# Compressive-memory attention on one core: the memory matrix in 32x32 blocks of two heads, q and k rows head by head

## The chip, the core and the metric

The kernel runs on one core of a Trainium2 chip. The metric is the device time of one execution in microseconds (us); lower is better. The core has a matrix engine (PE; PEld is its weight load), a vector engine (DVE), an activation engine (ACT), a general engine (POOL) and a sequencer that issues nearly all transfers (SP). The transfers run on 16 DMA engines.

## The reference, cut to what matters

One transformer block: adaptive layer norm, attention with a compressive memory, adaptive layer norm, a feed-forward network with GELU. 2048 rows, width 512, 32 heads of 16, four segments of 512 rows. The change touches only the attention.

```python
for s in range(4):                       # segments of 512 rows
    qs, ks, vs = q[:, :, s], k[:, :, s], v[:, :, s]
    a_dot = softmax(qs @ ks.T * scale + mask) @ vs       # within the segment
    pq = phi(qs)                                         # phi(t) = t + 1 if t > 0 else exp(t)
    num = einsum("bhld,bhde->bhle", pq, M)               # memory read-out, M is 16x16 a head
    den = einsum("bhld,bhd->bhl", pq, z)[..., None] + 1e-6
    o = g * num / den + (1 - g) * a_dot
    pk = phi(ks)
    M = M + einsum("bhld,bhle->bhde", pk, vs)            # memory update
    z = z + sum over l of pk
```

## The kernel before, in words

The program runs in three phases. Phase one, which the change touches, goes through the four segments: layer norm, projections to q, k and v, memory read-out and memory update. Phase two computes the dot-product attention of all heads and the output projection. Phase three is the feed-forward network.

**Order.** The order is written out by hand. For phase one it is the token lists `PRM['A']` (line 62), one for each segment, which the loop at line 531 turns into calls: `Q0` to `Q3` and `K0` to `K3` are projections of four groups of eight heads (128 rows: eight heads of 16) by 512 columns (the segment's rows); `R` is the read-out, `Rs`, `Rb`, `Rn`, `Ro` are the store of its reciprocal, the broadcast load of it, the multiplication and the store of the result; `Tk`, `Tc` and `U` transpose phi(k), copy it and update the memory. Segment 0 has no read-out. Each engine takes its instructions in the order in which the tokens emit them, and so does SP with its transfers. A transfer goes out on one of eight semaphore lanes in turn, so transfer n waits until transfer n-8 has landed.

**Projection** (`proj`, line 504). Twelve products on PE fill one PSUM bank of 128x512. ACT copies it, rounded, to a tile "hi" (line 516), DVE subtracts (line 517) and gives "lo"; each of the two has three buffers, so the copy of projection n waits until the stores of projection n-3 have landed. `store` (line 498) writes both to DRAM: hi goes to two planes of `QD` or `KD`, lo to the third. For the memory, ACT also makes exp (line 515), POOL or DVE clips it (line 520), and DVE joins the two halves of phi (line 526). The eight PSUM banks of the pool `psA` are used in turn by all tokens.

**Layout.** The columns of wq and wk are permuted on the host so that a group's row is `dim * 8 + head`. A plane of `QD[s][g]` in DRAM is `[dim 16][head 8][512]`, so hi and lo lie there exactly in the order of their 128 rows.

**Loads of phase two.** `load_stacks` (line 186) reads, for a "quad" Q of four heads, 48 rows of 4 KB for two of its heads at a time: two loads of k and two of q. A DRAM row of 4 KB is two neighbouring heads of one dim. The loads of quads 0 and 1 are emitted in segment 3 (token `B`), those of quad 2 right after the last store of phase one.

**Memory read-out** (`mem_read`, line 446). Four products give the denominators, four column blocks of 32 beside each other in one bank (`dn`, line 449). Then a product of 128 rows and 128 columns for each group g, with a 128x128 matrix M that is zero outside the blocks of its eight heads, gives the numerators in four banks (`nu`, line 457); ACT copies each to a tile `am`. DVE makes the reciprocals. `mem_store` writes them to DRAM (`rdd`), `mem_load` reads them back broadcast over 16 dims (`rb`, line 471), POOL multiplies (line 476), and `mem_out` stores the results to `AMD[s][g]` (line 480), from where phase two takes them.

**Memory update** (`mem_update`, line 426). For each group and each of four blocks of 128 rows a product of transposed phi(k) (128 columns) with 128 columns of V adds up in a bank `mp` (line 434); DVE multiplies with a mask of the heads (line 440) and adds the old M (line 443).

All of these memory products are in full fp32. The trace shows two weight loads and two products for each, so 16 products of `mp` are 32 rows in a segment.

Of the kernel before, what the change touches and what calls it, by code (L numbers as in the profile page):

```python
# [8 lines left out]
F32 = mybir.dt.float32  # L9
# [3 lines left out]
ALU = mybir.AluOpType  # L13
# [4 lines left out]
S, D, H, DH, NSEG, L, F = 2048, 512, 32, 16, 4, 512, 1792  # L18
# [4 lines left out]
VW = 17  # L23
# [81 lines left out]
def block_kernel(ctx: ExitStack, tc: tile.TileContext, x, wq, wk, wv, wo, betaq, betam,  # L105
                 w1, b1c, w2, b2, ccol, wmod, maskbd, mask8, out):
    nc = tc.nc
    v, act, pool, pe, sp = nc.vector, nc.scalar, nc.gpsimd, nc.tensor, nc.sync
# [3 lines left out]
    dram = ctx.enter_context(tc.tile_pool(name="dram", bufs=1, space=DRAM))  # L112
# [49 lines left out]

    QD = [[dram.tile([3, 16, 8, 512], F32, name=f"QD{s}_{g}") for g in range(4)] for s in range(NSEG)]
    KD = [[dram.tile([3, 16, 8, 512], F32, name=f"KD{s}_{g}") for g in range(4)] for s in range(NSEG)]
    TERMS = {"q": (slice(0, 3, 2), slice(1, 2)), "k": (slice(0, 2), slice(2, 3))}
    def home(Q):
        return Q % 5 if Q < 10 else (Q - 10) % 6

# [26 lines left out]
                    for p in range(2):  # L195
                        sp.dma_start(st[p][64 * h:64 * h + 48], rows[:, o + p, :])

    AMD = [[dram.tile([128, 512], F32, name=f"AMD{s}_{g}") for g in range(4)] for s in range(NSEG)]
    X2D = [dram.tile([128, 4, D], F32, name=f"X2D{s}") for s in range(NSEG)]
    GD = [[dram.tile([128, 512], F32, name=f"GD{s}_{f}") for f in range(FB)] for s in range(NSEG)]  # L200
    modD = dram.tile([6, D], F32, name="modD")
# [12 lines left out]
    V = [vp.tile([128, VROW], F32, tag="V", bufs=NB, name=f"V{b}") for b in range(NB)]  # L214
# [8 lines left out]
    with ExitStack() as pa:  # L223
        sa = pa.enter_context(tc.tile_pool(name="sa", bufs=2))
        wp = pa.enter_context(tc.tile_pool(name="wp", bufs=1))
        pp = pa.enter_context(tc.tile_pool(name="psA", bufs=8, space=PSUM))

        def pst(name):
            return pp.tile([128, 512], F32, tag="ps", name=name)

        def sat(tag, name, dt=F32):
            return sa.tile([128, 512], dt, tag=tag, bufs=PRM["bufs"][tag], name=name)
# [3 lines left out]
        def load_x(s):  # L236
            xs[s] = wp.tile([128, 4, D], F32, tag="xs", bufs=2, name=f"xs{s}")
            if s > 0:
                sp.dma_start(xs[s], xrows(s))
            else:  # L240
                for b in range(4):
                    (sp if b < 2 else act).dma_start(xs[0][:, b], xrows(0)[:, b])
# [32 lines left out]
        wvs = load_w(wvp, wv, "wv", "pkt")  # L275
        (wqh, wql), (wkh, wkl), (wvh, wvl) = wqs[:2], wks[:2], wvs[:2]
        load_x(1)
        mbd = wp.tile([128, 128], F32, name="mbd")
        m8 = wp.tile([128, 32], F32, name="m8")
        sp.dma_start(mbd, maskbd)  # L280
        sp.dma_start(m8, mask8)
# [55 lines left out]
        ps = pst("mpsa")  # L337
        for k in range(KB):
            for c in range(2):
                pe.matmul(ps[32 * c:32 * c + 32, :], sc[:, k:k + 1].to_broadcast([128, 32]), wms[c, k],  # L340
                          start=(k == 0), stop=(k == KB - 1))
        row = sat("pkt", "mrowa")
# [65 lines left out]

        mem = {"M": None, "z": None}
        phq, phk, zss, pks, mrd = {}, {}, {}, {}, {}  # L410
# [15 lines left out]
        def mem_update(s):  # L426
            z = zss[s]
            if mem["z"] is not None:
                v.tensor_tensor(out=z, in0=mem["z"], in1=z, op=ALU.add)
            mp = pst(f"mp{s}")  # L430
            for g in range(4):
                for b in range(4):
                    rhs = V[4 * s + b][:, VW * 8 * g:VW * 8 * g + VW * 8].rearrange("p (h c) -> p h c", c=VW)[:, :, :16]
                    pe.matmul(mp[:, 128 * g:128 * g + 128], pks[s][b][:, 128 * g:128 * g + 128], rhs,
                              start=(b == 0), stop=(b == 3))
            zm = sa.tile([128, 4, 32], F32, tag="zm", name=f"zm{s}")
            for g in range(4):
                v.tensor_scalar(zm[:, g, :], m8, z[:, g:g + 1], None, op0=ALU.mult)
            M = sa.tile([128, 4, 128], F32, tag="M", name=f"M{s}")
            v.tensor_tensor(out=M, in0=mp.rearrange("p (g n) -> p g n", g=4),  # L440
                            in1=mbd[:, :].unsqueeze(1).to_broadcast([128, 4, 128]), op=ALU.mult)
            if mem["M"] is not None:
                v.tensor_tensor(out=M, in0=M, in1=mem["M"], op=ALU.add)
            mem["M"], mem["z"], mem["zm"] = M, z, zm

        def mem_read(s):
            dn = pst(f"dn{s}")
            for g in range(4):
                pe.matmul(dn[32 * g:32 * g + 32, :], mem["zm"][:, g, :], phq[s, g], start=True, stop=True)
            rd = sa.tile([128, 512], F32, tag="rd", bufs=1, name=f"rd{s}")  # L450
            v.tensor_scalar(rd, dn, 1e-6, None, op0=ALU.add)
            v.reciprocal(out=rd, in_=rd)
            v.tensor_scalar(rd, rd, gm[:, 0:1], None, op0=ALU.mult)
            ams = []
            for g in range(4):
                ps = pst(f"nu{s}_{g}")
                pe.matmul(ps, mem["M"][:, g, :], phq[s, g], start=True, stop=True)
                am = sat("am" if s < 3 else "phk", f"am{s}_{g}")
                act.activation(am, ps, AF.Copy)
                ams.append(am)  # L460
            mrd[s] = [rd, ams, []]

        def mem_store(s):
            rdd = dram.tile([128, 512], F32, name=f"rdd{s}")
            sp.dma_start(rdd, mrd[s][0])
            mrd[s][0] = mem["r"] = rdd

        def mem_load(s):
            for g in range(4):
                rb = sat("pkt", f"rb{s}_{g}")  # L470
                sp.dma_start(rb, mrd[s][0][32 * g:32 * g + 8, :].unsqueeze(1).to_broadcast([8, 16, 512]))
                mrd[s][2].append(rb)

        def mem_mul(s):
# [1 line left out]
                pool.tensor_tensor(out=am, in0=am, in1=rb, op=ALU.mult)  # L476

        def mem_out(s):
            for g, am in enumerate(mrd[s][1]):
                sp.dma_start(AMD[s][g], am)  # L480

        def v_rows(ps, h, b, ks):
            for k in ks:
# [12 lines left out]
                l.pop(0)()  # L496

        def store(parts, nm, dd):
            rows = dd.rearrange("c r e n -> (r e) c n")
            for t, c in zip(parts, TERMS[nm]):  # L500
                d = rows[:, c]
                sp.dma_start(d, t.bitcast(F32).unsqueeze(1).to_broadcast([128, d.shape[1], 512]))

        def proj(s, nm, g):
            dd = (QD if nm == "q" else KD)[s][g]
# [104 lines left out]
    with ExitStack() as pb:  # L610
# [426 lines left out]
        for Q in range(-LEAD // 2, NP // 2 + 1):  # L1037
# [3 lines left out]
            for tok in ORDER.split():  # L1041
                if tok[0] == "c":
                    n = int(tok[1:])
# [3 lines left out]
                P, h = 2 * Q + int(tok[2]) // 2, int(tok[2]) % 2  # L1047
# [15 lines left out]
    with ExitStack() as pc:  # L1063
# [256 lines left out]
        for p in range(2):  # L1320
            n = FH * p + FH - 1
# [56 lines left out]
        for p in range(2):  # L1378
            for j in range(FH):
                quad(FH * p + j, j == 0)  # L1380
            n = FH * p + FH - 1
# [3 lines left out]
            for m in range(NM):  # L1385
                s, f = 2 * p + m // FB, m % FB
# [68 lines left out]
```

## Time and profile before

| what | value |
|---|---|
| median of 3 runs | 779.76 us (777.67 to 780.3) |
| the profiled execution | 786.26 us |
| its span, first to last instruction | 784.5 us |
| mean granted TensorE clock | 0.987 |
| PE busy | 773.5 us (99%) |
| DVE busy | 564.9 us (72%) |
| ACT busy | 456.6 us (58%) |
| POOL busy | 258.1 us (33%) |
| DMA | 156.28 MB, mean 199 GB/s |

The profile is a page on one execution, and a trace that can be asked for more. The views used here: the span in slices; sums over stretches of the span (busy time of each engine, then the mean granted clock, then "DMA share", the mean busy share of the 16 DMA engines, and what they moved in GB/s; a share slightly over 1 means that packets overlap); who waited for whom; groups of instructions by source line; instructions in order of time, neighbours of the same kind merged. All times count from the span's start.

### The profile page before, as it was taken

How to read it: one execution, taken by the hardware profiler on the slowest of the kernel's cores; microseconds unless marked ns; L12 is line 12 of the kernel's file. 1: busy time of each engine (PE TensorE's matmuls, PEld its weight loads, DVE VectorE, ACT ScalarE, POOL GpSimd, SP SyncE). 2: the span in 40 equal slices, each digit the busy share in tenths (PEclk: the TensorE clock that was granted, in tenths of full speed). 3: DMA queues.
4: the chain of work that ended last, by engine and by line, in shares of the span. 5: the costliest groups of instructions: out<-in, count | busy, mean ns of one | idle time of the engine just before them, and what ended most of it. 6: DMA issues, size and time to landing. Idle time of an engine off the chain costs nothing.

```text
span 784.5 us, 14474 instructions
## 1 busy us (share of the span) xinstructions
PE 773.5 (99%) x4532; PEld 541.2 (69%) x4532; DVE 564.9 (72%) x1686; ACT 456.6 (58%) x918; POOL 258.1 (33%) x437
## 2 busy tenths in 40 slices
PE   9999999999999999999999999999999999999998
PEld 4887787866555445555555547788878888888887
DVE  6765696449999889999988889868569764432424
ACT  3543444443888667777788676767644446652221
POOL 2205143410468445566665662242000404200000
PEclk9999999999999779999999999999999999999999
DMA  9777755396587677878777755595676524545543
GB/s 337 268 258 262 281 213 200 144 315 196 136 195 183 164 169 185 228 206 228 185 201 209 214 167 158 195 303 177 201 232 207 191 94 163 173 147 167 172 127 115
DMA packets 97376, 156.28 MB, mean 199 GB/s; under 512 B 15552, under 2 KB 31296, under 8 KB 97300
## 3 DMA queue, kind: packets, MB, share of 16 engines
q1 hardware_dynamic: 96436, 153.79, 63.6%
q10 hardware_dynamic: 864, 1.57, 0.6%
q8 instruction: 36, 0.59, 0.3%
q14 instruction: 40, 0.33, 0.1%
HBM read 93.95 MB, written 60.83 MB: 197 GB/s over the span
## 4 chain that ended last, share of the span: by engine, by line
PE 83%; DVE 5%; DMA 5%; ACT 3%; issue 2%; SPq 1%; POOL 0%; ACTq 0%; DVEq 0%; POOLq 0%
PE bx L1102 9%; PE att L723 8%; PE pv L751 7%; PE att L649 5%; PE q L334 5%; PE bx L1372 5%; PE bv L1102 5%; PE k L334 5%; PE by L1372 4%; PE bv L1372 4%; PE v L485 4%; PE mm L839 4%; PE spare L1372 2%; PE by L1102 2%; PE mm L751 2%
## 5 line engine op out<-in xcount | busy, mean ns | idle before, releaser
L637 DVE CUSTOM_DVE_ANT_0 dump<-att,maskb 128x512 bf16<-128x512 f32 (+3 forms) x512 | 220.2, 487 | 22.5 <-PE att L649 12.9
L723 PE MATMUL att<-qst,kst 50*128 50x512 f32 (+3 forms) x512 | 137.2, 378 | 2.6 <-DVE nm L637 2.2
L649 PE MATMUL att<-kst,qst 48*128 48x512 f32 (+3 forms) x512 | 122.7, 352 | 0.1
L723 PEld LDWEIGHTS att<-qst,kst 50*128 50x128 f32 x512 | 79.5, 191 | 62.1 <-DVE nm L637 47.6
L649 PEld LDWEIGHTS att<-kst,qst 48*128 48x128 f32 x512 | 77.7, 192 | 19.5 <-ACT ptc L726 8.5
L726 ACT ACTIVATE pta<-att 128x512 f32<-128x512 f32 x128 | 69.2, 592 | 32.2 <-PE att L723 25.1
L726 ACT ACTIVATE ptb<-att 128x384 f32<-128x384 f32 x128 | 62.9, 492 | 23.8 <-PE att L649 18.2
L883 POOL TENSOR_TENSOR wb<-wa 128x256 f32<-128x256 f32 x24 | 20.3, 847 | 152.4 <-DMA wa<-in_w 152.4
L708 POOL TENSOR_SCALAR_AFFINE_SELECT pta<-pta 128x256 f32<-128x256 f32 x64 | 27.2, 425 | 104.2 <-ACT pta L726 102.4
L726 ACT ACTIVATE ptc<-att 128x384 f32<-128x384 f32 x128 | 57.2, 492 | 0.9 <-PE att L723 0.9
L139 DVE TENSOR_TENSOR gl<-s,gh 128x512 fp32r<-128x512 f32 x34 | 24.1, 708 | 43.0 <-ACT gh L136 42.9
L708 POOL TENSOR_SCALAR_AFFINE_SELECT ptc<-ptc 128x256 f32<-128x256 f32 x128 | 52.0, 422 | 1.6 <-ACT ptc L726 0.5
L136 ACT ACTIVATE gh<-s 128x512 fp32r<-128x512 f32 x34 | 21.3, 628 | 47.7 <-DMA s<-GD 15.9
L1107 ACT ACTIVATE s<-s,b1t 128x512 f32<-128x512 f32 x42 | 30.3, 722 | 21.5 <-DVE s L1111 21.5
L1111 DVE TENSOR_TENSOR s<-bv,s 128x512 f32<-128x512 f32 x28 | 19.3, 689 | 32.1 <-PE bv L1102 22.3
L637 DVE DVE_READ_ACCUMULATOR2_ANT nm<- 128x1 f32 x512 | 42.2, 82 | 0.0
L708 POOL TENSOR_SCALAR_AFFINE_SELECT ptb<-ptb 128x256 f32<-128x256 f32 x64 | 26.9, 420 | 34.7 <-ACT ptb L726 34.7
L520 POOL TENSOR_SCALAR qp<-qp 128x512 f32<-128x512 f32 x12 | 18.5, 1546 | 42.9 <-ACT qp L515 42.9
L751 PE MATMUL pv<-pta,V 128*32 128x512 f32 x208 | 29.4, 639 | 0.5 <-ACT ms L130 0.5
L139 DVE TENSOR_TENSOR w1ml<-s,w1mh 128x512 fp32r<-128x512 f32 x18 | 13.0, 720 | 21.9 <-ACT w1mh L136 21.9
L751 PE MATMUL pv<-ptc,V 128*32 128x256 f32 (+1 forms) x416 | 28.1, 344 | 0.0
L136 ACT ACTIVATE w1mh<-s 128x512 fp32r<-128x512 f32 x18 | 11.3, 629 | 26.0 <-PE spare L1372 11.6
(378 smaller groups left out, 2078.7 us busy)
## 6 DMA issues: line engine op xcount, KB each, us to landing
GD<-s SPq DMA_DIRECT2D x56, 256.0 KB
s<-GD SPq DMA_DIRECT2D x52, 256.0 KB
kst<-KD SPq DMA_DIRECT2D x58, 192.0 KB
qst<-QD SPq DMA_DIRECT2D x58, 192.0 KB
QD<-q SPq DMA_DIRECT2D x16, 512.0 KB
KD<-k SPq DMA_DIRECT2D x16, 512.0 KB
TD<-ts SPq DMA_DIRECT2D x32, 256.0 KB
xt<-X2D SPq DMA_DIRECT2D x28, 256.0 KB
```

Source lines behind the costliest of these rows:

```text
L136: act.activation(hi, src, AF.Copy)
L139: lo_eng.tensor_tensor(out=lo, in0=src, in1=hi.bitcast(F32), op=ALU.subtract)
L334: pe.matmul(ps, a[:, k, 128 * g:128 * g + 128], b[k], start=(k == 0 and i == 0), stop=(k == KB - 1 and i == 2))
L485: pe.matmul(ps, a[k][:, 128 * b:128 * b + 128], w[:, k, :], start=(k == 0 and i == 0), stop=(k == KB - 1 and i == 2))
L637: v.tensor_tensor_reduce(out=dump[n_dump[0] % 2][:, :n], in0=src, in1=maskb[:, 512 - n:], scale=-1.0, scalar=-4 * NEG, op0=ALU.add, op1=AL ...
L649: pe.matmul(ps[:, o:o + n], q[:, 128 * i:128 * i + 128], k[:, :n], start=True, stop=True)
L708: pool.affine_select(out=t, in_=t, pattern=pattern, compare_op=ALU.is_ge, fill=0.0, base=0, channel_multiplier=-1)
L723: pe.matmul(ps[:, o:o + n], k[:, 128 * j:128 * j + 128], q[:, 128 * j:], start=True, stop=True)
L726: act.activation(pt[:, h, :], ps[:, :m], AF.Exp, scale=0.25)
L751: pe.matmul(ps[32 * c:32 * c + 32, lo:hi], V[4 * s + j][:, VW * hd:VW * hd + 32], pt[:, c // 2, lo - o:hi - o], start=start, stop=stop)
L1102: pe.matmul(ps, a[:, i, k, :], b[k], start=start and k == 0 and c == 0, stop=k == 1 and c == 2, skip_group_check=not start)
L1372: pe.matmul(ps, a[:, c], w[:, lo:hi], start=(f == 0 and i == 0), stop=(last and i == 2))
```

## The change

The host no longer permutes wq and wk, so a group's row becomes `head * 16 + dim`. Four things follow from that.

1. `store`: the DRAM tensors `QD` and `KD` keep their layout `[dim][head][512]`, so the 128 rows of a tile go to eight heads (outer) by 16 dims (inner). Each plane gets a transfer of its own: three transfers of 256 KB in place of one of 512 KB and one of 256 KB.
2. `mem_update`: of each group only the four 32x32 blocks of two neighbouring heads are computed. Each product of 128 by 128 columns becomes four of 32 by 32 columns, which go to the partitions 32r of one bank. M shrinks from 128x4x128 to 128x4x32, its mask to 128x32, and the two DVE operations on it with them.
3. `mem_read`: sixteen products of 32 rows and 32 columns take the place of four of 128 rows and 128 columns. Product (g, r) sits at row block 32r and column block 32g of the array and writes partitions 32g of bank r. A bank now holds head pair r of all four groups, and so do the tiles `am` and `rb`. All four banks are taken ahead of the products, and the copies by ACT come behind all sixteen.
4. The transfers of the read-out follow the new order: the reciprocals go to DRAM in four transfers of eight rows (segments 1 and 2), and `am` goes to `AMD` as four groups (outer) of 32 rows.

```diff
-    TERMS = {"q": (slice(0, 3, 2), slice(1, 2)), "k": (slice(0, 2), slice(2, 3))}
+    TERMS = {"q": ((0, 2), (1,)), "k": ((0, 1), (2,))}
...
-    AMD = [[dram.tile([128, 512], F32, name=f"AMD{s}_{g}") for g in range(4)] for s in range(NSEG)]
+    AMD = [dram.tile([4, 128, 512], F32, name=f"AMD{s}") for s in range(NSEG)]
...
-                    rhs = V[4 * s + b][:, VW * 8 * g:VW * 8 * g + VW * 8].rearrange("p (h c) -> p h c", c=VW)[:, :, :16]
-                    pe.matmul(mp[:, 128 * g:128 * g + 128], pks[s][b][:, 128 * g:128 * g + 128], rhs,
-                              start=(b == 0), stop=(b == 3))
+                    for r in range(4):
+                        h = VW * (8 * g + 2 * r)
+                        rhs = V[4 * s + b][:, h:h + 2 * VW].rearrange("p (h c) -> p h c", c=VW)[:, :, :16]
+                        pe.matmul(mp[32 * r:32 * r + 32, 32 * g:32 * g + 32],
+                                  pks[s][b][:, 128 * g + 32 * r:128 * g + 32 * r + 32], rhs, start=(b == 0), stop=(b == 3))
...
-            M = sa.tile([128, 4, 128], F32, tag="M", name=f"M{s}")
-            v.tensor_tensor(out=M, in0=mp.rearrange("p (g n) -> p g n", g=4),
-                            in1=mbd[:, :].unsqueeze(1).to_broadcast([128, 4, 128]), op=ALU.mult)
+            M = sa.tile([128, 4, 32], F32, tag="M", name=f"M{s}")
+            v.tensor_tensor(out=M, in0=mp[:, :128].rearrange("p (g n) -> p g n", g=4),
+                            in1=mbd[:, :].unsqueeze(1).to_broadcast([128, 4, 32]), op=ALU.mult)
...
+            nu = [pst(f"nu{s}_{r}") for r in range(4)]
             for g in range(4):
-                ps = pst(f"nu{s}_{g}")
-                pe.matmul(ps, mem["M"][:, g, :], phq[s, g], start=True, stop=True)
-                am = sat("am" if s < 3 else "phk", f"am{s}_{g}")
+                for r in range(4):
+                    pe.matmul(nu[r][32 * g:32 * g + 32, :], mem["M"][32 * r:32 * r + 32, g, :], phq[s, g][32 * r:32 * r + 32, :],
+                              start=True, stop=True, tile_position=(32 * r, 32 * g))
+            for r, ps in enumerate(nu):
+                am = sat("am" if s < 3 else "phk", f"am{s}_{r}")
                 act.activation(am, ps, AF.Copy)
                 ams.append(am)
...
-            rdd = dram.tile([128, 512], F32, name=f"rdd{s}")
-            sp.dma_start(rdd, mrd[s][0])
+            if s < 3:
+                rdd = dram.tile([4, 4, 2, 512], F32, name=f"rdd{s}")
+                for g in range(4):
+                    sp.dma_start(rdd[:, g], mrd[s][0][32 * g:32 * g + 8, :])
+            else:
+                rdd = dram.tile([128, 512], F32, name=f"rdd{s}")
+                sp.dma_start(rdd, mrd[s][0])
...
-            for g in range(4):
-                rb = sat("pkt", f"rb{s}_{g}")
-                sp.dma_start(rb, mrd[s][0][32 * g:32 * g + 8, :].unsqueeze(1).to_broadcast([8, 16, 512]))
+            for r in range(4):
+                rb = sat("pkt", f"rb{s}_{r}")
+                sp.dma_start(rb, mrd[s][0][r].rearrange("g h n -> (g h) n").unsqueeze(1).to_broadcast([8, 16, 512]))
...
-            for g, am in enumerate(mrd[s][1]):
-                sp.dma_start(AMD[s][g], am)
+            for r, am in enumerate(mrd[s][1]):
+                sp.dma_start(AMD[s][:, 32 * r:32 * r + 32, :], am)
...
-            rows = dd.rearrange("c r e n -> (r e) c n")
-            for t, c in zip(parts, TERMS[nm]):
-                d = rows[:, c]
-                sp.dma_start(d, t.bitcast(F32).unsqueeze(1).to_broadcast([128, d.shape[1], 512]))
+            for t, cs in zip(parts, TERMS[nm]):
+                for c in cs:
+                    sp.dma_start(dd[c].rearrange("r e n -> e r n"), t.bitcast(F32))
...
-        "wq": head_rows(A_wq),
-        "wk": head_rows(A_wk),
+        "wq": A_wq,
+        "wk": A_wk,
```

On SP, from the last projections of segment 1 to the first store of segment 2. In the rows below, KD and QD are the DRAM planes of k and q, rdd and rb the reciprocals out and back, AMD the read-out; the shape is what the transfer writes. Before:

```order
L502 DMA KD1_3_96<-k01_3_1028 128x2x512 [waits DMAHW0_49,Activation_49]
L502 DMA KD1_3_96<-k11_3_1029 128x512 [waits DMAHW1_49,DVE_49]
L239 DMA xs3_1096<-in_x 128x4x512 [waits DMAHW2_49]
L465 DMA rdd1_1098<-rd1_1043 128x512 [waits DMAHW3_49,DVE_49]
L471 DMA rb1_0_1116<-rdd1_1098 128x1x512 [waits DMAHW4_49,DMAHW3_49]
L471 DMA rb1_1_1118<-rdd1_1098 128x1x512 [waits DMAHW5_49]
L471 DMA rb1_2_1120<-rdd1_1098 128x1x512 [waits DMAHW6_49]
L471 DMA rb1_3_1122<-rdd1_1098 128x1x512 [waits DMAHW7_49]
L480 DMA AMD1_0_109<-am1_0_1049 128x512 [waits DMAHW0_49,Pool_49]
```

The same place now:

```order
L511 DMA KD1_3_96<-k01_3_1078 8x16x512 [waits DMAHW7_49,Activation_49]
L511 DMA KD1_3_96<-k01_3_1078 8x16x512 [waits DMAHW0_49]
L511 DMA KD1_3_96<-k11_3_1079 8x16x512 [waits DMAHW1_49,DVE_49]
L239 DMA xs3_1160<-in_x 128x4x512 [waits DMAHW2_49]
L472 DMA rdd1_1162<-rd1_1094 4x2x512 [waits DMAHW3_49,DVE_49]
L472 DMA rdd1_1162<-rd1_1094 4x2x512 [waits DMAHW4_49]
L472 DMA rdd1_1162<-rd1_1094 4x2x512 [waits DMAHW5_49]
L472 DMA rdd1_1162<-rd1_1094 4x2x512 [waits DMAHW6_49]
L481 DMA rb1_0_1183<-rdd1_1162 128x1x512 [waits DMAHW6_49,DMAHW5_49,DMAHW7_49,DMAHW4_49,DMAHW3_49]
```

Three more rows of `rb` follow, and then these, with the first store of segment 2 behind them:

```order
L490 DMA AMD1_106<-am1_0_1118 4x32x512 [waits Pool_49]
L490 DMA AMD1_106<-am1_1_1120 4x32x512 [waits Pool_49]
L490 DMA AMD1_106<-am1_2_1122 4x32x512 [waits Pool_49]
L490 DMA AMD1_106<-am1_3_1124 4x32x512 [waits Pool_49]
L511 DMA QD2_0_81<-q02_0_1369 8x16x512 [waits DMAHW7_49,Activation_49]
```

The order of the steps is the same; a store of a projection writes as 8x16 rows what it wrote as 128 rows, in one transfer more, and the read-out writes as 4x32 rows what it wrote as 128.

On ACT, the copy of the second projection in segment 2 (line 516 before, 525 now) shows the wait for the stores of three projections ahead. Before, then now:

```order
L515 ACTIVATE qp2_1_1287<-q2_1_1272 128x512 [waits PE_49]
L516 ACTIVATE q02_1_1285<-q2_1_1272 128x512 [waits DMAHW6_49]
L515 ACTIVATE qp2_2_1314<-q2_2_1299 128x512 [waits PE_49]
L516 ACTIVATE q02_2_1312<-q2_2_1299 128x512 [waits DMAHW0_49]
L515 ACTIVATE qp2_3_1339<-q2_3_1324 128x512 [waits PE_49]
```

```order
L524 ACTIVATE qp2_1_1402<-q2_1_1387 128x512 [waits PE_49]
L525 ACTIVATE q02_1_1400<-q2_1_1387 128x512 [waits DMAHW5_49,DMAHW4_49]
L524 ACTIVATE qp2_2_1430<-q2_2_1415 128x512 [waits PE_49]
L525 ACTIVATE q02_2_1428<-q2_2_1415 128x512 [waits DMAHW7_49,DMAHW0_49]
L524 ACTIVATE qp2_3_1456<-q2_3_1441 128x512 [waits PE_49]
```

Nothing is moved here; the copy waits for two transfers where it waited for one.

More of the change, by code (lines that the diff above doesn't have):

```diff
@@ L277, in block_kernel @@
         load_x(1)
-        mbd = wp.tile([128, 128], F32, name="mbd")
+        mbd = wp.tile([128, 32], F32, name="mbd")
         m8 = wp.tile([128, 32], F32, name="m8")
@@ L1416 @@
     from concourse.bass_utils import run_bass_kernel_spmd
-    def head_rows(w):
-        w = np.asarray(w).reshape(D, 4, 8, 16)
-        return np.ascontiguousarray(w.transpose(0, 1, 3, 2).reshape(D, D))
     beta = np.asarray(A_beta).reshape(4, 8)
@@ L1424 @@
     betam[:, :8] = beta
-    row = np.arange(128)
-    head_of_row = row % 8
+    head_of_row = np.arange(128) // 16
     a = {
         "x": np.asarray(A_x).reshape(S, D),
-        "wq": head_rows(A_wq),
-        "wk": head_rows(A_wk),
+        "wq": A_wq,
+        "wk": A_wk,
         "wv": A_wv,
@@ L1440 @@
         "wmod": w_mod,
-        "maskbd": (head_of_row[:, None] == (np.arange(128) // 16)[None, :]).astype(np.float32),
+        "maskbd": (head_of_row[:, None] % 2 == (np.arange(32) // 16)[None, :]).astype(np.float32),
         "mask8": (head_of_row[:, None] == np.arange(32)[None, :]).astype(np.float32),
```

## The prediction

> **What bounds the kernel now.** I read the page first, then sums over stretches of phase one, then the order of time.
>
> ```profile
> span 784.5 us, 14474 instructions
> PE   9999999999999999999999999999999999999998
> DMA  9777755396587677878777755595676524545543
> ```
>
> PE is busy in every slice, so what PE doesn't have to do is gained, and what it has to wait for is lost. But the DMA row is fullest in the first slices, which are phase one. What phase one stores, and two of its loads (number of transfers, size of each):
>
> ```profile
> QD<-q SPq DMA_DIRECT2D x16, 512.0 KB
> KD<-k SPq DMA_DIRECT2D x16, 512.0 KB
> ...
> QD<-q SPq DMA_DIRECT2D x16, 256.0 KB
> KD<-k SPq DMA_DIRECT2D x16, 256.0 KB
> ...
> AMD<-am SPq DMA_DIRECT2D x12, 256.0 KB
> rb<-rdd SPq DMA_DIRECT2D x8, 256.0 KB
> ...
> rdd<-rd SPq DMA_DIRECT2D x3, 256.0 KB
> ```
>
> Phase one by stretches (busy us of each engine, the granted clock, the DMA share, GB/s):
>
> ```profile
> 26.00:54.00 28.00, 28.00 (x149) 23.98 (x148) 18.55 (x42) 14.48 (x29) 5.75 (x5) 1.00 0.94 338
> 54.00:62.00 8.00, 8.00 (x42) 5.71 (x41) 7.30 (x17) 2.88 (x5) 1.11 (x1) 1.00 0.00 2
> 62.00:91.00 29.00, 29.00 (x124) 20.80 (x123) 20.66 (x38) 12.82 (x23) 10.78 (x9) 1.00 0.93 335
> 91.00:106.00 15.00, 15.00 (x100) 13.42 (x99) 7.69 (x16) 6.20 (x12) 5.23 (x4) 1.00 0.38 142
> 106.00:131.00 25.00, 25.00 (x106) 17.50 (x105) 20.30 (x37) 12.34 (x23) 12.61 (x10) 1.00 0.73 262
> 131.00:152.00 21.00, 21.00 (x126) 18.43 (x125) 9.79 (x20) 7.99 (x14) 5.09 (x4) 1.00 0.31 115
> 152.00:184.00 32.00, 31.32 (x132) 21.34 (x130) 17.97 (x42) 15.41 (x23) 5.92 (x4) 1.00 0.91 306
> ```
>
> While q and k are projected the DMA engines are busy for 0.73 to 0.94 of the time; in between they idle. Where nothing is left over, the projections already wait:
>
> ```profile
> 167.53 0.60 ACT L516 ACTIVATE k<-k 128x512 fp32r<-128x512 f32 x1 [5.75 <-DMA QD<-q]
> ```
>
> ACT's copy of a projection waits 5.75 us for the stores of three projections ahead; PE only just stays busy, its banks being the reserve. So phase one is bound by PE with the transfers close behind: what makes stores dearer uses up the idle stretches, then holds PE.
>
> **What a store costs.** Two stretches, with stores of 128 rows and with the four loads `rb`, whose DRAM side is 8 rows, each read 16 times:
>
> ```profile
> 78.00:84.00 6.00, 6.00 (x25) 3.09 (x24) 4.96 (x12) 3.94 (x7) 1.70 (x1) 1.00 1.05 408
> 95.00:97.00 2.00, 2.00 (x10) 1.59 (x10) 0.00 (x0) 0.83 (x2) 1.15 (x1) 1.00 0.49 189
> ```
>
> With 128 rows the engines are full (1.05) and move 408 GB/s: 256 KB (262,144 bytes) take 0.64 us. With four `rb` queued, none waiting for another, the share stays at 0.49 and the rate at 189 GB/s: half of the engines move them, and 256 KB take 1.39 us. That is the row that decides. The changed stores have 8x16 rows of 2 KB on the DRAM side, outermost 8, as `rb` has. I take it that they, too, keep half of the engines, 1.39 us each.
>
> [...]
>
> **The change part by part.**
>
> *Stores of q and k.* 16 + 16 of 512 KB and 16 + 16 of 256 KB are 96 units of 256 KB, before and after. Each occupies the engines it uses for 1.39 in place of 0.64 us: 96 x 0.75 = 72 us more. Below, nothing more, if all engines take part. Above, the loads of weights from 36 to 40 us are the nearest slower row:
>
> ```profile
> 36.00:40.00 4.00, 4.00 (x20) 3.30 (x19) 3.13 (x8) 1.81 (x4) 1.49 (x1) 1.00 0.99 308
> ```
>
> Half the engines at that pace, 154 GB/s, would take 1.70 us, and 96 x 1.06 = 102 us more. I take 72, by the row with the same shape.
>
> *Stores of the read-out.* Twelve units. Halves give 12 x 0.75 = 9 us. Quarters would be twice the 1.39, an estimate from that row: 2.77 us, so 12 x 2.13 = 25.6 us more. Bounds 0 and 25.6. I take 25.6: from 128 rows to 8 the engines halved, and 4 is half of 8.
>
> *Stores of the reciprocals.* Three of 256 KB are 1.9 us; in segments 1 and 2 only 32 rows are left. About 1.9 us less at most. But `rb` waits on SP for four landings, and `AMD` and the next segment's first stores stand behind it on SP:
>
> ```profile
> 88.73 0.32 SPq L465 DMA_DIRECT2D rdd<-rd  x1
> 91.55 2.56 SPq L471 DMA_DIRECT2D rb<-rdd  x4
> ```
>
> From the issue of `rdd` to that of `rb` pass 2.8 us, in which the queue may run empty; twice, 5.6 us. It was so before, but then there was idle time.
>
> *Sum over the engines.* Share times length of the seven stretches: 26.3 + 0 + 27.0 + 5.7 + 18.3 + 6.5 + 29.1 = 112.9 us of work from 26 to 184. With 72 + 25.6 - 1.9 it is 208.6 us for the lowest engines, more than the 158 us there are. The stretches in which they idled fill up; from 26 on that ends at 234.6, and with the 5.6 us of empty queue near 240. As the share can stand at 1.05, it may be up to 10 us less.
>
> *What waits for it.* Three buffers of hi and lo hold it together: ACT's copy waits for both hi stores of three projections ahead, DVE's subtraction for the lo store. Behind ACT's copy stand the next exp and the copies to `am` and V; behind DVE's, the joins of phi. The banks stay taken, and PE waits. On SP, the loads of quad 2 stand behind the last stores:
>
> ```profile
> 178.81 1.59 SPq L193 DMA_DIRECT2D kst<-KD  x2
> 180.46 0.92 SPq L193 DMA_DIRECT2D qst<-QD  x2
> ```
>
> ```profile
> 192.18 0.67 PE L649 MATMUL att<-kst,qst 48*128 48x512 f32 x3
> ```
>
> They land by about 184, and PE's first product of quad 2 is at 192.18, so 8 us of slack are there. Now they land at 230 to 240: PE is late by 38 to 48 us. I take 46, nearer the upper end, as the empty moments come on top. The rest of the span is as before.
>
> *Read-out on PE.*
>
> ```profile
> 80.34 1.06 PE L449 MATMUL dn<-qp,zm 128*32 128x512 f32 x8
> 81.34 3.70 PE L457 MATMUL nu<-qp,M 128*128 128x512 f32 x8
> 84.48 0.80 PE L485 MATMUL v<-wvh,Ahh 128*128 128x512 f32 x1
> ```
>
> The eight rows of `nu` take 81.34 to 84.48, 3.14 us. `dn` shows what blocks side by side do: eight products in 1.0 us, four column blocks at once. Sixteen blocks at once would be near 1.0 us (2.1 less); four rounds of the kind of `dn`, 4.0 us (0.9 more). I take 1.0.
>
> *Update on PE and DVE.*
>
> ```profile
> 52.53 3.74 PE L434 MATMUL mp<-V,pk 128*128 128x128 f32 x32
> 56.03 0.48 PE L334 MATMUL q<-Ahh,wqh 128*128 128x512 f32 x1
> 475.21 0.83 PE L751 MATMUL att<-ptc,V 128*32 128x128 f32 x16
> L440 DVE TENSOR_TENSOR M<-mp,mbd 128x512 f32<-128x512 f32 x3 | 2.0, 683 | 0.0
> L443 DVE TENSOR_TENSOR M<-M,M 128x512 f32<-128x512 f32 x2 | 1.8, 910 | 0.1
> ```
>
> The 32 rows of `mp` take 3.5 us; now there are 128 with a quarter of the columns. If four blocks run at once, 0.9 us; if each takes its 52 ns as the narrow weights of phase two do (0.83 us for 16), 6.7 us. I take 3.5, between. DVE's two operations shrink to a quarter, 2.9 us less in all. PE waits for banks 46 us in phase one, so none of this moves the end; without that wait it would be 2.1 us a segment to gain, and up to 3.2 us to lose.
>
> *No cost:* the copies to `am` behind all products (four of 0.6 us, ending about when they did, since the products end sooner); the four banks taken ahead; the host's order of the weights.
>
> **Against the clock.** The profiled execution took 786.26 us (span 784.5 and 1.76 around it), 6.5 over the median of 779.76. 46 us on it is 832; on the median, 826.
>
> **The rivals.**
>
> *A: the forecast*, half the engines for q and k, a quarter for `AMD`: 38 to 48 us late and some us for the estimate of the quarter, 818 to 832, chance 0.60.
>
> *B: AMD keeps eight engines or all sixteen.* 16.6 to 25.6 us less work, so 20 to 30 us late in place of 46: 800 to 811. For it: no row shows a four, and 32 neighbouring rows are 64 KB in one piece that could be split. 0.16.
>
> *C, the other side: all engines take part.* The order of the rows is on the DRAM side alone, and the rows shown with a share of 0.49 are loads that read each row 16 times; it could be the repeated reading that halves the rate. Then the stores cost 0.64 us as before, and PE has less to do: 2.1 us of `nu` and up to 2.6 of `mp`, three times each, 6 to 14 us: 766 to 774. It decides if the share of the engines stands near 1 while a queue of stores moves. Against it: repeated reads that were only slow would show a full share at a low rate, as here:
>
> ```profile
> 160.00:164.00 4.00, 4.00 (x19) 3.34 (x18) 2.49 (x4) 1.78 (x4) 2.94 (x2) 1.00 1.00 207
> ```
>
> Those loads of the stacks are slow with all engines busy; `rb` is slow with half of them idle. 0.07.
>
> *D: each engine is slower at the scattered stores,* as at the weights above: 102 in place of 72 us, so up to 30 us beyond A: 840 to 856. For it: 2 KB rows 16 KB apart. Against it: the share of `rb` fits the 408 GB/s halved. 0.08.
>
> *F: the small products hold PE as well.* The weight load of `dn`, as narrow as theirs, lasts 107 ns:
>
> ```profile
> L449 PEld LDWEIGHTS dn<-qp,zm x24: 106/108/109, 80.3 to 169.5; 128*32 128x32 f32 x24
> ```
>
> Were it not overlapped, 128 of them would be 13.7 us a segment in place of 3.5, three times 10 us more, of which half or more falls in PE's waits: 830 to 841. Against it: the 52 ns of phase two. 0.03.
>
> *E: the buffers hide more than I think,* or the projections wait less often: 780 to 800. 0.05; the 5.75 us wait above says that there is no reserve.
>
> *The change doesn't do what it says:* if the blocks don't run side by side, `nu` stays at 3 to 4 us, and the time is A's.
>
> **How the numbers follow.** The chances are A 0.60, B 0.16, C 0.07, D 0.08, E 0.05, F 0.03, and 0.01 for no change at all. 0.3% (2.3 us) is about what a measurement of this kernel can tell from no change. Faster: C, 0.07. Same: 0.02, from C's and E's edges. Slower: 0.91. The likeliest is A: 826. From 800 to 850 lie A, B, F and more than half of D; C, E and the rest of D, with no change some 0.16, are left out.
>
> **What would show it.** Right: a DMA share near 0.5 in stretches where QD stores queue, lower yet with `AMD`; ACT's copies waiting for DMA in all segments, PE waiting for ACT or banks in phase one; the first product of quad 2 near 238 us; `nu` near 1 us. Wrong: a share near 1 in those stretches, PE without gaps before 190 us, or a gap that ends with PE's own small products.

## The result, and the profile after

| what | before | after |
|---|---|---|
| median | 780.03 us (777.67 to 781.43, 4 runs) | 833.21 us (831.76 to 835.13, 4 runs) |
| the profiled execution | 786.26 us | 831.76 us |
| its span | 784.5 us | 830.0 us |
| first product of quad 2 | 192.18 us | 237.37 us |
| mean granted TensorE clock | 0.987 | 0.966 |

The change makes the kernel 6.9% slower: ratio 1.0687, 95% interval 1.0652 to 1.0721. The forecast was 826 us, the range 800 to 850. Ratios leave out executions more than 1.5% above the fastest of the same kernel (among the experiments one of twelve in best and four of twelve in best_v3); the medians given are of all.

The page of the changed kernel, engines over the span:

```profile
span 830.0 us, 15250 instructions
PE   9979797895859999999999999999999999999998
PEclk9999899897969998999999999999999999999999
DMA  9476535455437777777877775468666634545453
```

PE has holes in the first third, and the DMA row, which began with 9777, now has half-full digits where q and k are stored. The sums of three stretches (busy us of each engine, granted clock, DMA share, GB/s), two with stores of q or k alone and one with stores of the read-out:

```profile
28.00:40.00 12.00, 12.00 (x55) 9.94 (x54) 4.58 (x13) 3.05 (x8) 2.99 (x2) 1.00 0.51 184
203.00:212.00 9.00, 8.07 (x61) 4.63 (x29) 5.77 (x6) 5.06 (x8) 0.00 (x0) 0.93 0.53 204
172.00:176.00 4.00, 4.00 (x19) 3.28 (x18) 3.89 (x9) 2.31 (x5) 3.83 (x4) 1.00 0.26 94
```

I read a share of 0.51 to 0.53 while stores queue as half of the engines at work, and 0.26 as a quarter; the views give the mean of the 16. At these rates 256 KB take 1.29 us (204 GB/s) and 2.79 us (94 GB/s). The outermost count on the DRAM side is 8 for the first and 4 for the second.

Who waits for whom in the first 260 us, on ACT and on PE (us in total, times, longest):

```profile
ACT k L525 <- DMA QD<-q: 38.8, 11, 8.1
...
ACT q L525 <- DMA QD<-q: 21.5, 3, 10.0
```

```profile
PE dn L451 <- DVE qp L535: 11.7, 3, 7.6
PE att L658 <- DMA qst<-QD: 9.9, 1, 9.9
PE v L495 <- DVE kp L535: 5.5, 2, 2.7
```

ACT's copies wait 60 us for stores of q. In the kernel before, from 26 to 186 us, they wait 12 us for them:

```profile
ACT k L516 <- DMA QD<-q: 12.0, 6, 5.7
```

Behind them DVE's joins of phi come late, and PE waits for these. Phase one ends for PE at the wait of 9.89 us for quad 2's stack:

```profile
237.37 1.60 PE L658 MATMUL att<-kst,qst 48*128 48x512 f32 x3 [9.89 <-DMA qst<-QD]
```

That is 45.2 us later than before's 192.18, and all of the difference between the two profiled spans (45.5 us). From this product to the end they are alike, 592.32 and 592.63 us:

```profile
192.18:784.50 592.32, 583.69 (x3626) 400.42 (x3625) 437.08 (x1400) 369.68 (x771) 207.38 (x360) 0.98 0.63 183
```

```profile
237.37:830.00 592.63, 582.98 (x3625) 401.92 (x3625) 435.92 (x1396) 369.04 (x769) 205.38 (x360) 0.98 0.63 183
```

The products themselves became much shorter. Read-out and update in the changed kernel:

```profile
86.20 1.05 PE L460 MATMUL nu<-qp,M 32*32 32x512 f32 x6
88.86 1.13 PE L460 MATMUL nu<-qp,M 32*32 32x512 f32 x26 [1.61 <-DVE kp L535]
...
110.03 1.48 PE L436 MATMUL mp<-V,pk 128*32 128x32 f32 x128
111.44 0.50 PE L334 MATMUL q<-Ahh,wqh 128*128 128x512 f32 x1
```

The 128 rows of the update take 1.41 us where 32 rows took 3.5. PE's gap inside `nu` shows that the time saved lies in a place where PE waits.

### The profile page after: what moved, and what is told of

It is laid out like the page before. It is cut to its first block, busy times and chain, and to the rows that moved or that the text cites. A ratio compares the mean times of both kernels' runs of the same rounds, so it can differ in the third digit from the quotient of the medians.

```text
span 830.0 us, 15250 instructions
## 1 busy us (share of the span) xinstructions
PE 778.0 (94%) x4892; PEld 538.5 (65%) x4892; DVE 566.9 (68%) x1686; ACT 455.0 (55%) x918; POOL 256.7 (31%) x437
## 4 chain that ended last, share of the span: by engine, by line
PE 65%; DMA 15%; DVE 9%; issue 4%; ACT 3%; SPq 2%; POOL 1%; ACTq 0%; DVEq 0%; POOLq 0%
PE bx L1111 8%; PE att L732 7%; PE pv L760 6%; DMA QD<-q 6%; PE q L334 5%; PE bx L1381 5%; PE att L658 4%; PE bv L1111 4%; PE by L1381 4%; PE bv L1381 4%; PE mm L848 4%; PE v L495 3%; PE spare L1381 2%; DVE dump L646 2%; DMA qst<-QD 2%
## 5 line engine op out<-in xcount | busy, mean ns | idle before, releaser
L732 PE MATMUL att<-qst,kst 50*128 50x512 f32 (+3 forms) x512 | 135.5, 373 | 2.3 <-DVE nm L646 1.9
L526 DVE TENSOR_TENSOR k<-k,k 128x512 fp32r<-128x512 f32 x16 | 11.1, 691 | 42.1 <-DMA QD<-q 35.4
L525 ACT ACTIVATE k<-k 128x512 fp32r<-128x512 f32 x16 | 9.6, 597 | 48.7 <-DMA QD<-q 38.8
L526 DVE TENSOR_TENSOR q<-q,q 128x512 fp32r<-128x512 f32 x16 | 11.0, 688 | 27.6 <-DMA QD<-q 19.3
```

The source lines that it names most:

```text
L732: pe.matmul(ps[:, o:o + n], k[:, 128 * j:128 * j + 128], q[:, 128 * j:], start=True, stop=True)
```

## The experiments

The theories: 1, the number of engines follows the outermost count of a transfer; 2, rows scattered in DRAM are slow to write; 3, the small products hold PE.

### Stores of 8x16 or 16x8 rows, nothing else changed: pad8 and pad16

```diff
-    QD = [[dram.tile([3, 16, 8, 512], ...
+    QD = [[dram.tile([3, 8, 17, 512], ...        # pad16: [3, 16, 9, 512]
-                sp.dma_start(d, t.bitcast(F32)...            # d: 128 rows, one or two planes
+                sp.dma_start(dd[i, :, :16], t.bitcast(F32))  # pad16: dd[i, :, :8]; one plane each
```

KD is changed alike. The rows keep the order of before. The loads of pad8 follow the padding with 24x2 rows in place of 48.

Expected of pad8:

> The kernel before, its memory matrix and read-out untouched; only the DRAM planes of q and k are padded (8 pieces of 17 rows, the last row of each unused), so that each store is one of 256 KB whose DRAM side is 8x16 rows of 512. The 16 rows of a piece lie next to each other, nothing is scattered. Theory 1 (the number of engines follows the outermost count): stores show a DMA share near 0.5 and about 1.25 us each, 96 x 0.6 = 58 us more work for the engines used, 15 to 25 us slower than before: 795 to 805. Theory 2 (rows scattered 16 KB apart are slow to write): as before, 778 to 783. Theory 3 (the blocks of the memory matrix hold PE): as before, too.

Expected of pad16:

> As pad8, but 16 pieces of 9 rows: the DRAM side of a store is 16x8 rows, with the same three transfers a projection and the same kind of gaps. Theory 1: all engines, 0.64 us a store, 778 to 783. If it were padding, gaps or the third transfer that cost, it would be as slow as pad8.

Measured: pad8 819.74 us, ratio 1.0527 (1.0476 to 1.0577); pad16 781.56 us, ratio 1.001 (0.9976 to 1.0044). Nine stores of k on SP's queue, with eight lanes full, first pad8, then pad16 (start, duration):

```profile
189.71 10.31 SPq L501 DMA_DIRECT2D KD<-k  x9
```

```profile
170.69 6.21 SPq L501 DMA_DIRECT2D KD<-k  x9
```

From issue to issue a store takes 1.15 us against 0.69. The rate in this stretch of pad8:

```profile
191.00:200.00 9.00, 8.33 (x21) 4.04 (x22) 3.28 (x6) 3.16 (x6) 0.00 (x0) 0.79 0.53 204
```

Rows that lie next to each other move at the same share and rate, 0.53 and 204 GB/s, as the scattered rows of the changed kernel do; pad16 has 1.06 and 406 GB/s from 170 to 176 us. The third transfer and the gaps cost next to nothing (pad16's first product of quad 2 comes 2.5 us after before's); the outermost count does. A share of 1.06 at 16 rows and of 0.53 at 8 is what theory 1 expects; theory 2 falls as a cause, and the prediction's rival D with it. The first product of quad 2, pad8 and then pad16:

```profile
222.68 0.76 PE L648 MATMUL att<-kst,qst 48*128 48x512 f32 x1 [5.22 <-DMA qst<-QD]
```

```profile
194.72 0.51 PE L648 MATMUL att<-kst,qst 48*128 48x512 f32 x2
```

28.0 us, more than the 15 to 25 expected, and pad8's median lies 15 us above the 805 that I gave as its upper end. A small part of the 28 us belongs to the loads, which had changed shape too: those of quads 0 and 1 hold SP for 7.5 us in place of 4.5. The rest of its span is 603 us in place of 585; 12.8 us of that are PE's busy time, at a granted clock of 0.97 in place of 1.00, and 4.7 us are waits, so I count none of it as the stores' doing.

### The read-out's stores in pieces: amd32

```diff
-                sp.dma_start(AMD[s][:, 32 * r:32 * r + 32, :], am)
+                for g in range(4):
+                    sp.dma_start(AMD[s][g, 32 * r:32 * r + 32, :], am[32 * g:32 * g + 32, :])
```

> The changed kernel with one edit: each store of the read-out goes out as four of 32 rows, one a head group, in place of one of 4x32 rows. Theory 1: the 12 stores of 2.8 us each on a quarter of the engines become 0.64 us of all, 25 us less work on the lowest engines; phase one ends 20 to 26 us earlier, 807 to 815. Theory 2 and 3: no change from the changed kernel, 830 to 836.

Measured: 823.5 us, ratio to before 1.0563 (1.0504 to 1.0622), and in the trace:

```profile
227.72 0.76 PE L659 MATMUL att<-kst,qst 48*128 48x512 f32 x1 [4.36 <-DMA qst<-QD]
```

9.65 us earlier than the changed kernel, not 20 to 26, and the median lies 8.5 us above the 815 that I gave as its upper end. The quarter is real (the share of 0.26 shown above), but a good part of it lies where the queue has room: in segment 1 the changed kernel's stores of `AMD` move at a share of 0.31 while PE is busy without a gap.

```profile
117.00:121.00 4.00, 4.00 (x19) 3.33 (x18) 2.96 (x4) 2.00 (x4) 4.00 (x4) 1.00 0.31 86
```

The first four stores, those of segment 1, gain some 1 us (segment 2's last nine stores of k begin at 146.20 against 147.29 us). The second four stand ahead of the loads of quads 0 and 1 and the nine stores of q behind these. Those stores on SP, in the changed kernel and then in amd32:

```profile
191.03 10.26 SPq L511 DMA_DIRECT2D QD<-q  x9
```

```profile
185.45 10.23 SPq L512 DMA_DIRECT2D QD<-q  x9
```

With these stores 5.6 us of the 9.65 are reached; the other 4 come behind the last four stores, ahead of the loads of quad 2.

### The stores of q and k in 128 rows, the loads in pieces: qk128

```diff
-    QD = [[dram.tile([3, 16, 8, 512], ...
+    QD = [[dram.tile([3, 8, 16, 512], ...
-                    sp.dma_start(dd[c].rearrange("r e n -> e r n"), t.bitcast(F32))
+                    sp.dma_start(dd[c].rearrange("e r n -> (e r) n"), t.bitcast(F32))
...
+                for c in range(3):    # a load of 48 rows becomes three of 16
```

> The changed kernel with its stores of q and k as 128 rows next to each other in DRAM (planes of 8 heads by 16 dims); the loads of phase two then take three pieces of 16 rows where they took one of 48. The stores of the read-out stay 4x32 rows. Theory 1: 96 x 0.6 = 58 us or more leaves the low engines, the 26 us of the read-out fill idle stretches: 768 to 785, with the first product of quad 2 near 190 us. Theory 2 (scatter): the same, as nothing of q and k is scattered. Theory 3: 825 or more.

Measured: 880.03 us, ratio 1.1266 (1.1228 to 1.1304): far off. Phase one went the way that theory 1 said, though not all of it: quad 2's first product comes 36 us earlier than in the changed kernel, and 12 us after the 190 expected (the loads of quads 0 and 1, in 24 pieces, hold SP from 155 to 169 us, where pad16's eight take 4.5 us):

```profile
201.68 0.76 PE L659 MATMUL att<-kst,qst 48*128 48x512 f32 x1 [5.12 <-DMA qst<-QD]
```

But three times as many loads in phase two hold SP's queue, and PE waits there, over the whole span:

```profile
PE att L733 <- DMA qst<-ms: 22.9, 9, 5.1
PE att L659 <- DMA qst<-QD: 18.3, 10, 5.1
```

From quad 2 to the end it takes 679 us in place of the changed kernel's 593: 38 us more are idle time of PE, and 49 us are PE's busy time, at a granted clock of 0.88 in place of 0.98 (over the whole profiled executions 0.901 and 0.966). As a test of the whole time this run is spoilt by its own repair. The next ones repair the stores and keep the loads' number and size; only the order of the rows within a load changes.

### Rows pair by pair: pair, best, and the control pairold

The weights' columns, permuted on the host, give a row the place `pair * 32 + dim * 2 + head of the pair`. A block of 32 rows still holds two heads, and a plane is stored in 128 rows in one piece.

```diff
+    def pair_rows(w):
+        w = np.asarray(w).reshape(D, 4, 4, 2, 16)
+        return np.ascontiguousarray(w.transpose(0, 1, 2, 4, 3).reshape(D, D))
...
-    QD = [[dram.tile([3, 16, 8, 512], ...
+    QD = [[dram.tile([3, 4, 16, 1024], ...       # a row of 1024 is the two heads of a pair
-            rows = dd[s][g].rearrange("c r e n -> (c r) e n")
+            rows = dd[s][g].rearrange("c e r n -> r c e n")
```

`pair` is the changed kernel with this, `best` has the edit of amd32 as well, `pairold` is the kernel before (its 128x128 products) with this. Expected:

> The changed kernel with a group's rows ordered pair by pair, and in a pair dim by dim with its two heads side by side. The blocks of 32 rows hold the same two heads, all the products of the changed kernel stay, but a store of q or k is 128 rows in one piece of DRAM, in two transfers a projection as before, and the loads of phase two keep their size. The stores of the read-out stay 4x32 rows. Theory 1 (engines by the outermost count): the 58 us or more of the q and k stores are gone; the 26 us of the read-out lie mostly in idle stretches: 768 to 782. Theory 2 (scattered rows are slow) gives the same for q and k. Theory 3 (the small products hold PE): 825 or more.

> As pair, and each store of the read-out goes out as four of 32 rows. Theory 1: no transfer of phase one but the reciprocals is left on part of the engines; what remains is the saving of PE, 2.1 us a read-out and 2.1 us an update (1.4 in place of 3.5 us), three times each, as far as PE does not wait: 766 to 776, and 0 to 8 us under pair. Theory 3: as pair, 825 or more.

> The kernel before with the pair order of the rows and the DRAM planes of pair and best, and its own 128x128 products of the memory: the control for best. Theory 1 and 2: 778 to 783, so that best's distance to it is the worth of the blocks alone. If the loads of phase two in their new order (16 dims outermost, then 3 planes) cost or save something, it shows here.

Measured: pair 788.42 us, ratio 1.0103 (1.0056 to 1.015); best 788.13, 1.0077 (1.0046 to 1.0108); pairold 783.76, 1.0034 (1.0006 to 1.0063). All three lie above what I expected, best by 12 us. The first product of quad 2 in pair, best and pairold:

```profile
194.81 0.46 PE L659 MATMUL att<-kst,qst 48*128 48x512 f32 x1 [1.62 <-DMA qst<-QD]
```

```profile
190.97 0.50 PE L660 MATMUL att<-kst,qst 48*128 48x512 f32 x2
```

```profile
193.51 0.51 PE L649 MATMUL att<-kst,qst 48*128 48x512 f32 x2
```

So the 45.2 us of phase one come apart: the q and k stores 42.6 (237.37 to 194.81), the read-out's stores 3.8 beyond that (to 190.97), the blocks -2.5 (best against pairold), the pair order +1.3 (pairold against before). The parts hold in this order only, and each is the difference of two profiled executions: while the stores of q and k are slow, those of the read-out are worth 9.65 us (amd32), and the half engines alone cost 28.0 us (pad8). Theory 3 is gone. But best is not faster than before, though I had expected it to be. Up to quad 2 its PE is busy 8.3 us less than pairold's (181.2 against 189.5 us) and idle 5.8 us more (9.8 against 4.0), so 2.5 us are left; 5.2 us of its waits are for splits of a segment's input into hi and lo. In best the q products behind the update of segment 1 begin 4.5 us earlier than in pairold (98.28 against 102.82 us), and then:

```profile
97.06 1.30 PE L436 MATMUL mp<-V,pk 128*32 128x32 f32 x128
...
100.13 0.50 PE L334 MATMUL q<-Ahh,wqh 128*128 128x512 f32 x1 [0.88 <-DVE Ahh L138]
...
101.81 0.49 PE L334 MATMUL q<-Ahl,wqh 128*128 128x512 f32 x1 [0.94 <-DVE Ahl L139]
...
103.22 0.79 PE L334 MATMUL q<-Ahh,wqh 128*128 128x512 f32 x1 [0.92 <-DVE Ahh L138]
```

PE waits for the splits of the next segment's input, which DVE makes beside POOL's multiplications, and some of them slowly:

```profile
98.58 1.50 DVE L138 CAST Ahh<-Ah 128x512 fp32r<-128x512 f32 x1
100.11 1.64 DVE L139 TENSOR_TENSOR Ahl<-Ah,Ahh 128x512 fp32r<-128x512 f32 x1
```

```profile
98.21 4.68 POOL L486 TENSOR_TENSOR am<-am,rb 128x512 f32<-128x512 f32 x3 [0.55 <-ACT Ah L318]
```

### Where the saving of PE goes: best_rm, best_v3 and their controls

best_rm moves POOL's multiplication and the stores behind it into the next segment, best_v3 moves the last product of V behind the transposes, for PE to have work during the splits. Token lists of segment 1 and the next:

```diff
-  ... Tc V3 At Ah H U Rn     |  Q0 Ro s0 D D Q1 s1
+  ... Tc V3 At Ah H U        |  Q0 Rm s0 D D Q1 Ro s1       best_rm, old_rm
+  ... Tc At Ah H V3 U Rn     |  Q0 Ro s0 D D Q1 s1          best_v3, old_v3
```

> As best, but POOL's multiplication of the read-out and the stores behind it stand one and two projections later, in the next segment, so that POOL does not work while DVE splits the next segment's input. Theory P (what the blocks save on PE is given back in waits for those splits, which take 1.5 to 1.65 us each beside POOL in place of 0.42 and 0.69): the splits are short again, the gaps ahead of PE's first q products of segments 2 and 3 (2.7 and 1.8 us in best) shrink below 1 us, the first product of quad 2 comes 3 to 6 us before best's 190.97 us, the time is 3 to 6 us under best's 788. Theory R (the saving is lost elsewhere, in the later phases): within 2 us of best.

> The control: the same two moves in pairold, which has the 128x128 products. Its PE reaches the q products 4.5 us later and does not wait for the splits: within 2 us of pairold's 784 by both theories; by theory P best_rm is then level with it or up to 4 us faster.

> As best, but the last product of V of a segment (2.8 us of PE) stands behind the transposes for the next segment, in front of the update, so that PE works while DVE splits. Theory P: the gaps ahead of the q products shrink, less a wait of up to 0.7 us for ACT's copy of V ahead of the update; 2 to 5 us under best. Theory R: within 2 us of best.

> The control for best_v3: the same move in pairold. Theory P and R: within 2 us of pairold's 784, or up to 2 us slower by the wait for ACT's copy of V.

Measured: best_rm 787.24 us, ratio to before 1.0075 (1.0046 to 1.0105); old_rm 792.46, 1.0166 (1.013 to 1.0202); best_v3 784.24, 1.0013 (0.998 to 1.0047); old_v3 787.71, 1.0083 (1.0051 to 1.0116).

In best_rm the splits are short again, as theory P has it, and PE's waits for them fall from 5.2 to 0.7 us:

```profile
98.79 0.42 DVE L138 CAST Ahh<-Ah 128x512 fp32r<-128x512 f32 x1
99.25 0.69 DVE L139 TENSOR_TENSOR Ahl<-Ah,Ahh 128x512 fp32r<-128x512 f32 x1
```

But the moved multiplication now stands on POOL ahead of clips of q, and PE has a new wait in segment 3:

```profile
PE dn L451 <- DVE qp L537: 8.5, 1, 8.5
```

Its first product of quad 2 comes at 194.88 us, 3.9 us after best's, not 3 to 6 before it, and its time is the one that theory R gave, 0.9 us under best. As the new wait is longer than what there was to gain, I count it for neither theory. old_rm, 8.7 us slower than pairold, shows the same move costing where nothing was to gain, against what I had expected of it.

In best_v3 the waits for the splits fall to 1.8 us, but the update now waits 3.7 us for ACT's copy of V, where I had allowed 0.7. Phase one ends 1.4 us before best's. The time is 3.9 us under best in the medians (expected 2 to 5) and 5 us by the ratios, so most of that lead lies behind quad 2, where the two kernels have the same instructions (last section), and it does not show theory P. old_v3 waits 3.4 us for V, and is 3.9 us slower than pairold, 2 more than expected. The first product of quad 2, in best_v3 and then in old_v3:

```profile
189.56 0.51 PE L660 MATMUL att<-kst,qst 48*128 48x512 f32 x2
```

```profile
195.24 0.51 PE L649 MATMUL att<-kst,qst 48*128 48x512 f32 x2
```

With PE busy during the splits the blocks are worth 5.7 us of phase one (189.56 against 195.24), and 3.5 us in the medians, but against a control that the move itself slows. Against pairold, without the move, best_v3 is level: ratios of 1.0013 and 1.0034, with intervals that overlap. It is level with before, too; none of the runs is faster than before. That the splits take part of the saving is shown by PE's waits; that their removal makes the kernel faster is not shown.

## Why the prediction was right

**The store's price, half the engines.** Right in kind (shares of 0.51 to 0.53), a little too dear: 1.39 us taken from `rb`, 1.29 measured (204 GB/s). 96 x 0.65 = 62 us of work in place of 72.

**The quarter for the read-out.** The unit was right: 2.77 us estimated, 2.79 measured. The worth of it wasn't: I put all 25.6 us on the path (rival B, without it, was to be 20 to 30 us late in place of 46), and amd32 shows 9.65. The step that failed is the sentence that the idle stretches fill up: in segment 1 the share is 0.31 while PE has no gap. Why they do not fill no run isolates; that three buffers let only a few stores queue ahead is my guess.

**The empty moments.** I gave 2.8 us each to the way from `rdd` to `rb`. In the changed kernel:

```profile
101.41 2.59 SPq L472 DMA_DIRECT2D rdd<-rd  x4
110.21 2.51 SPq L481 DMA_DIRECT2D rb<-rdd  x4
```

8.8 us here, and 5.7 in segment 2. The queue of k stores ahead makes the way long, not the small pieces: in best, where k's stores move at a share of 1.05 (74 to 80 us), the same four pieces take 4.2 us in segment 1, and in pad8, where k's stores move at 0.53 (191 to 200 us) and `rdd` is one transfer of 128 rows, it is 8.0. That the stores of q, k and the read-out load the same engines, the "lowest" of my sum and of the expectations, no run shows; shown are mean shares of the 16, 0.53 and 0.26. On that assumption, work of 112.9 + 62 + 25.8 - 1.9 = 199 us ends at 237.4, 211 us after the first store, so by this estimate some 12 us are empty where I had 5.6. The two errors, 10 us too much work and 6 too little emptiness, nearly cancel, which is luck: 237.4 lies in the 230 to 240 that I gave, and the 45.2 us are the 46 of the forecast.

**Why the medians are 53 us apart and the profiles 45.** The profiled execution of before was 6.2 us over its median, that of after 1.5 under. The forecast put 46 on the median; the 7 us to the 833 measured I read as the late phases, where the change has no instruction: they take 592.32 us in the profiled execution of before, and 585.18 in pad16 with the same instructions (last section). No execution of before near its median was profiled, so this is argued, not shown.

**The update on PE.** I took 3.5 us, half way; it is 1.4. The guess hid behind PE's waits, as the text said, and cost nothing. These are 40 us, near the 46 that I had: some 24 behind DVE's joins of phi (`dn`, `v`, `nu` and the transposes of phi(k)), 9.9 for quad 2's stack. Not all are waits for banks, as I had put it: the transposes read the joined phi.

**The other side, rival C.** Its premise fell, the share is 0.53 and not near 1. Its price was wrong as well: with k's stores at a share of 1.05 best isn't 6 to 14 us faster, but level or slower. Of the 8.3 us that PE is busy less in phase one, waits take back 5.8, most of them for DVE's splits, and the 2.5 that are left don't reach the median. (B's range should have ended at 810, not 811, by its own terms.)

## What to carry to other kernels

Before rows are reordered so that a product gets smaller, write down the shape of every transfer that follows and look at its outermost count on the DRAM side: here queued stores moved at a DMA share of 1.06 at 16, 0.53 at 8 and 0.26 at 4. The four stores at 4 were cheap in segment 1, where the queue had room (some 1 us), and dearer ahead of the loads with which the next phase begins (some 4 us for each of the other two fours). And when work is taken off the busiest engine, look at what its next instruction waits for: here 5.8 of 8.3 us came back as waits, most of them for conversions and subtractions on DVE.

## What the runs showed of the hardware that I had not expected

**PE's clock after a gap.** In the changed kernel, 6 us with few products and the 6 us behind them:

```profile
86.00:92.00 6.00, 2.39 (x36) 0.37 (x32) 2.38 (x6) 2.17 (x4) 1.48 (x1) 0.96 0.53 203
92.00:98.00 6.00, 5.27 (x12) 4.13 (x13) 3.87 (x10) 2.56 (x5) 0.00 (x0) 0.50 0.53 204
```

The product behind the longest gap:

```profile
92.73 0.80 PE L495 MATMUL v<-wvh,Ahh 128*128 128x512 f32 x1 [2.74 <-DVE kp L535]
```

Behind it the granted clock is 0.50, and products start 0.43 us apart in place of 0.23, until 98.0 us. The gaps ahead are of 1.61 and 2.74 us, with 1.1 us of products between them; in best three gaps of 0.9 us within 5 us (shown above) also end in products 0.43 us apart. So these waits of PE were paid for twice, as work was ready behind them: the twelve products from 92.73 to 98.02 us take 5.3 us in place of 2.7.

**The clock of the late phases.** From quad 2 to the end, in pad16, best and best_v3, with the same instructions:

```profile
194.72:779.90 585.18, 575.98 (x3626) 398.66 (x3625) 434.34 (x1400) 368.50 (x771) 206.61 (x360) 1.00 0.63 185
```

```profile
190.97:786.60 595.63, 582.08 (x3626) 401.69 (x3625) 433.94 (x1400) 368.99 (x771) 205.16 (x360) 0.98 0.63 182
```

```profile
189.56:775.80 586.24, 575.07 (x3626) 399.20 (x3625) 429.47 (x1400) 368.77 (x771) 205.48 (x360) 0.99 0.63 185
```

There are 10.5 us of difference, with mean granted clocks of 1.00 to 0.98; 6 of them are PE's busy time. The low clock lies in one stretch or two, as here in the kernel before and then in best, where PE has hardly a gap:

```profile
262.00:270.00 8.00, 7.94 (x42) 3.38 (x45) 6.13 (x29) 4.86 (x12) 3.43 (x7) 0.58 0.64 145
```

```profile
294.00:302.00 8.00, 8.00 (x45) 3.76 (x45) 3.44 (x15) 3.83 (x9) 4.98 (x9) 0.50 0.80 192
```

What sets this off no run here settles. It goes with the kernel, though: the mean granted clock of best's twelve executions lies between 0.976 and 0.989, that of pairold's twelve between 0.991 and 0.998 (part of this is phase one, 0.99 against 1.00 in the two profiles). The medians of best and pairold differ by 4.4 us the other way than their phase one does; I put that down to the late phases, 595.63 us in best's profile and 587.49 in pairold's, but no run isolates it.

**DVE beside POOL.** In best a conversion of 128x512 on DVE takes 0.42 us alone (103.81 us) and up to 1.50 us while POOL multiplies (98.58 us), a subtraction 0.69 (104.26 us) and up to 1.64 (100.11 us). best_rm, which keeps the two apart, has 0.42 to 0.43 and 0.69 us in all four splits from 97.72 to 102.07 us. Not every one is slowed: in pairold a conversion at 99.08 us takes 0.43 us, though POOL multiplies from 95.30 to 100.63.
